# A transformer block whose TensorE takes turns between attention rows, weighted sums and one dense product, with fewer re-layouts and other places for two small steps

## The chip, the cores and the metric

The kernel runs on one core of a Trainium2 chip. The metric is device time in microseconds (us) from the first to the last instruction's end as the launch sees it, the median of several runs. A core has five engines with instruction streams of their own, which wait for each other by semaphores: TensorE (PE: matmuls, with the loading of the stationary operand, PEld, beside them), VectorE (DVE), ScalarE (ACT), GpSimd (POOL) and SyncE (SP, which here only starts transfers). Sixteen DMA engines move data. PSUM, where TensorE writes, has eight banks of 128 partitions by 512 floats.

## The reference, cut

```python
# S=2048 rows, D=640, H=32 heads of Dh=20, window W=256, F=1536; float32; inputs about 0.05 * randn
def _A_ref(x, wqkv, wo):                       # x is already layer-normalised
    q, k, v = (x @ wqkv).reshape(B, S, 3, H, Dh).transpose(2, 0, 3, 1, 4)
    scores = einsum("bhqd,bhkd->bhqk", q, k) * Dh ** -0.5
    mask = (i - j >= 0) & (i - j < W)
    p = softmax(where(mask, scores, -1e9))
    return einsum("bhqk,bhkd->bhqd", p, v).transpose(0, 2, 1, 3).reshape(B, S, D) @ wo
def _B_ref(x, w_gate, w_up, w_down):
    return (gelu(x @ w_gate) * (x @ w_up)) @ w_down
h  = x + _A_ref(layernorm(x), wqkv, wo)
h2 = h + _B_ref(layernorm(h), w_gate, w_up, w_down)
```

## The kernel before, in words

**Precision.** Every operand of a dense product is split into a high and a low half in float16, and a product is the sum of three matmuls (high by high, high by low, low by high). With 640 = 5 x 128 rows of contraction, a product into one bank (`products`, L538) is 15 matmuls: 256 columns wide for q and k, 320 for v and the output projection `wo`, 512 for gate and up.

**Tiles.** The 2048 rows are 16 blocks of 128; two blocks are a chunk of 256 columns, so eight chunks. q and k come out of their products transposed (features on partitions). `qk_out` (L717) splits them into halves, and ScalarE's queue writes them to DRAM (`qk<-qks`). `stack` (L737) reads them back in the layout that attention needs: for each parity of head, at partitions 0 and 64, three groups of 20 partitions (the 20 features of a head), for q high, high, low and for k high, low, high, so that one contraction over 60 partitions gives the three-term product. These re-layouts are `qT<-qk` (two buffers, one per chunk, taken by turns) and `kT<-qk` (a ring of six blocks), both started in SP's queue. For chunk c of 2 and more the one for q waits until block 2c-3 has had its weighted sums (`scored`), since it overwrites the q of two chunks ago.

**Attention.** A block of 128 queries has eight units: a unit is a parity of head and four heads, against up to three blocks of keys. For each unit:

- `maxima` (L792): 12 matmuls with queries on partitions (`ps<-kT,qT`, 60 rows of contraction); then VectorE masks one block of keys by a predicated copy and reduces the maxima to `mxs` (`max_out`, L886). When all eight units have them, `max_rows` and `max_transpose` turn the maxima into two more rows of q (`mT`, written by two transfers `qT<-mT` in ScalarE's queue).
- `scores` (L804): 12 matmuls with keys on partitions (`ps<-qT,kT`, 62 rows, so that the maximum is subtracted), the exponential on ScalarE (`pt<-ps,esc`), and the causal masks on GpSimd.
- weighted sums (`value_lane`, L948): 12 matmuls `ps<-pt,v` into bank 7 (`PV`), a quarter of the bank for each unit, with a column of ones that yields the softmax's denominator. After four units ScalarE copies the bank to `oT`, and `normalise` (L973) turns it by four transposes into a free bank, where VectorE takes the reciprocal (`rec`) and multiplies (`o32`). After eight units `o_transpose` splits `o32` in halves (`turned`, L506: high by ScalarE into `sph`, low by VectorE into `spl`) and two transposing transfers `oh<-sph`, `ol<-spl` in SP's queue give the operand of `wo_block`. `turned` does the same for the layer norms' outputs (`xh`, `xl`, and `h0h`, `h0l` before the feed-forward part).

A row stretch (`row_lane`, L874) is one unit's maxima and another unit's scores, of opposite parity, whose matmuls alternate; it takes six of the PSUM banks (`SETS`: 0 to 2 and 3 to 5), and VectorE, or ScalarE, frees its three when it has read them. Bank 6 is for dense products.

**What sets the order.** All instructions are written out at build time by a planner. Each piece of work is a generator (a lane) that says on which engine its next instruction runs and from when it may; a model of the engines' times (`Clock`) says when that is. At each step the main loop (from L1335) takes the first lane of a list that may start. The list `order` puts small work first (outputs, transposes, side work) and then the three lanes that fill TensorE: `rows`, `values` and `dense` (the products of q, k, v, `wo`, and later the feed-forward part). Which of the three comes first depends on the share of dense work done against the share of scores done (`ahead`), and weighted sums come early where the last matmul was one of a row stretch (`nc.mode == "row"`). A lane keeps its place only for one instruction, so a product of 15 matmuls may be cut anywhere by the others. All instructions go through one helper, so in the profile they bear its line L192; what they are is told by the names of their tiles.

Of the kernel before, what the change touches and what calls it, by code (L numbers as in the profile page):

```python
# [22 lines left out]
NB = S // P  # L23
# [222 lines left out]
def block_kernel(ctx: ExitStack, tc: tile.TileContext, x, wqkv, wo, wg, wu, wd, out):  # L246
# [18 lines left out]
    def at_bank(i):  # L265
        return ps8[:, i * 512:(i + 1) * 512]
# [18 lines left out]
    def bank(kind, dt=F32):  # L285
        b = pick(kind)[1]
        held[b] = kind
        ap = at_bank(b)
        return ap if dt == F32 else ap.bitcast(dt)

    def done(ap):
        del held[nc.box(ap)[1][2] // BANK]
# [32 lines left out]
    FFBACK = dict(split_lane=0.4, scale_lane=0.4, chunk_lane=0.3)  # L325
    EARLY = 0.6
    PACE = 1.0

    def need(*reads, slots=(), when=None, eng="tensor"):

# [6 lines left out]
    def pe(*reads, slots=(), when=None):  # L337
        return ("tensor",), need(*reads, slots=slots, when=when)

    def on(eng, *reads, when=None, after=None):  # L340
        f = need(*reads, when=when, eng=eng)
        if after is not None:
            return (eng,), lambda: max(f(), nc.others(after, eng))
        return (eng,), f
# [161 lines left out]
    def turned(src, lane, to, dst=None, when=None):  # L506

        yield on("scalar", src, when=lambda: not opened["parts"] and (not when or when()))
        opened["parts"] += 1
        hi, lo = (nc.tile(lnp, [P, D], F16, n, 1) for n in ("sph", "spl"))  # L510
        nc.scalar.copy(hi, src)
        yield on("vector", hi)
        nc.vector.tensor_tensor(lo, src, hi, op=ALU.subtract)
        if dst:
            to = dst()
        for o, i in zip(to, (hi, lo)):
            yield ("sync",), need(i, eng="sync")
            nc.sync.dma_start_transpose(o, i)
        opened["parts"] -= 1
# [18 lines left out]
    def products(n, term, ready=None, at_=None):  # L538


        ps = [at_[0]] if at_ else []
        col = at_[1] if at_ else 0

        def start(i):
            if ready and not ready(i):
                return INF
            t = nc.ready([x for ab in term(i) for x in ab], "tensor")
            return t if ps else max(t, room("mm"))

        for i in range(n):  # L550
            yield ("tensor",), lambda i=i: start(i)
            if not ps:
                ps.append(bank("mm"))
            m = term(i)
            for k, (l, r) in enumerate(m):
                if k:
                    yield pe()
                o = ps[0][:, col:col + r.free_size()]
                nc.tensor.matmul(o, l, r, start=(i == 0 and k == 0),
                                 stop=(i == n - 1 and k == len(m) - 1))  # L560
                pos["dense"] += r.free_size() * 3 // len(m)
        return o

    ffk = const.tile([P, FG, 5], F32, name="ffk")
# [172 lines left out]
    def stack(c, which, d):  # L737
        yield ("sync",), need(when=lambda: pos["consts"] and (c < 2 or B[2 * c - 3].scored),
                              eng="sync")
        if which == 0:  # L740
            C[c].qT = at("qT", [P, H // 2, CW], F16)
            for b in (2 * c, 2 * c + 1):
                B[b].mx = at("mxs", [P, H], F32, 4)
            to = C[c].qT
        else:
            s = 2 * c % RK
            to = kT[:, :, s:s + 2, :].rearrange("p i r n -> p i (r n)")
        for par in range(2):
            for m, i in enumerate(((0, 0, 1), (0, 1, 0))[which]):
                rows = slice(64 * par + DH * m, 64 * par + DH * m + DH)  # L750
                if c > 1:
                    yield ("sync",), lambda: nc.moved["sync"] - PACE
                nc.sync.dma_start(to[rows], d[i].rearrange("(a d i) n -> a d i n", a=2,
                                                           d=DH)[par])
        C[c].stacked += 1
        if C[c].stacked == 2:
            for b in (2 * c, 2 * c + 1):
                maxq.extend((b, u ^ 1) for u in range(H // 4))
            maxq.sort(key=lambda x: (x[0], x[1] // 2))
# [114 lines left out]
    def row_lane():  # L874
        while True:
            yield ("tensor",), row_need
            gens = []
            for s, (f, x) in enumerate(row):
                (maxq if f is maxima else scoreq).remove(x)
                gens.append(f(*x, row_set(s)))  # L880
            for ops in zip_longest(*gens):
                for op in ops:
                    if op:
                        nc.tensor.matmul(*op, start=True, stop=True)
# [63 lines left out]
    def value_lane():  # L948

        while True:  # L950
            yield pe(when=lambda: valq and B[valq[0][0]].v == 2 and pos["ones"])
            j, u = valq.popleft()
            b = B[j]
            pt = b.pt.pop(u)
            ks = window(j)
            n = len(ks)
            order = [1, 0, 2] if n == 3 else list(range(n))
            yield pe(pt[:, 3 - n:3], pv[:, u % 4, :])
            for k, i in enumerate(order):
                for c in range(4):  # L960
                    nc.tensor.matmul(pv[32 * c:32 * c + DH + 1, u % 4, :],
                                     vring[ks[i] % RV][:, 4 * u + c, :], pt[:, 3 - n + i, c, :],
                                     start=(k == 0), stop=(k == n - 1))
            pos["values"] += 1
            if u % 4 == 3:
                yield on("scalar", pv, when=lambda: pos["normal"] == 2 * j + u // 4)
                oT = at("oT", [P, 4, P], F32, 1)
                nc.scalar.copy(oT, pv)
                tps.append(normalise(j, u // 4, oT))
            if u == 7:  # L970
                b.scored = True

    def normalise(j, half, oT):  # L973
        b = B[j]
        yield pe(oT, slots=["tp"], when=lambda: j == 0 or half or B[j - 1].normal)
        if half == 0:
            b.o32 = at("o32", [P, H, DH], F32, 1)
        t = bank("tp")
        OR = 3 * 32 + DH + 1
        for u4 in range(4):  # L980
            nc.tensor.transpose(t[:, u4 * P:u4 * P + OR], oT[:OR, u4, :], ident[:OR, :OR])
        pos["normal"] += 1
        tv = t.rearrange("p (h e) -> p h e", e=32)
        rec = at("rec", [P, 16], F32)
        yield on("vector", t)
        nc.vector.reciprocal(rec, tv[:, :, DH])
        yield on("vector", rec)
        nc.vector.tensor_tensor(b.o32[:, 16 * half:16 * half + 16, :], tv[:, :, 0:DH],
                                rec[:, :, None].to_broadcast([P, 16, DH]), op=ALU.mult)
        done(t)  # L990
        pos["over"] = j == NB - 1 and half
        if half:
            tps.append(o_transpose(j))

# [340 lines left out]
    while dense.alive or sides or side or outs or tasks:  # L1335
        while side:
            back, gen = side.pop(0)
            sides.append(Lane(gen, back))
        while tps:
            trans.append(Lane(tps.pop(0), OUT))  # L1340
        while tasks:
            outs.append(Lane(tasks.pop(0), OUT))
        att_lanes = [rows, values]
        ahead = pos["dense"] / DENSE - pos["score"] / (H // 4) - TARGET
        early = [l for l in sides if l.gen.__name__ == "x_lane"] if not B[XF].ready else []
        if not W["v"].ready:
            att_first = maxq or nc.t["vector"] < nc.t["tensor"]
        else:
            att_first = ahead > 0
        if W["o", 0].ready:  # L1350
            outs.sort(key=lambda l: l.gen.__name__ == "low")
        if nc.mode == "row":
            early = [values] + early
        elif len(valq) < 2 and row_need() < INF:
            att_lanes = [rows]
        order = (early + outs + trans + sides
                 + (att_lanes + [dense] if att_first else [dense] + att_lanes))
        for lane in order:
            if lane.alive and lane.start(now):
                break  # L1360
        else:
            now += 0.03
            idle += 1
            assert idle < 20001, "nothing can be issued"
            continue
        idle = 0
        lane.step()
        trans = [l for l in trans if l.alive]
        outs = [l for l in outs if l.alive]
        sides = [l for l in sides if l.alive]  # L1370
# [48 lines left out]
```

## Time and profile before

| what | value |
|---|---|
| three runs | 1147.69, 1149.43, 1153.9 us; median 1149.43 |
| the profiled execution: time, span | 1152.97 us, 1151.0 us |
| mean granted TensorE clock | 0.966 |
| busy: PE, DVE, ACT, POOL | 1009.4 (88%), 636.6 (55%), 386.8 (34%), 195.3 us (17%) |
| attention beside projections | about 100 to 750 us of the span |
| feed-forward part (gate, up, down), from about 750 us on | 401 us |

Busy time counts an engine's work, not its waiting. A line of the waits gives: the operation that waited, an arrow, what ended its waiting, then the total in us, the number of times, and the longest. A line of the groups gives the operation with its tiles and shapes, the count, the busy time and the mean of one in ns, and then the idle time of the engine ahead of these operations with what ended most of it. DMA share is that of all sixteen engines. A line of the chain gives a start, a length and what filled it.

### The profile page before, as it was taken

Reading aid. Unit: us, or ns where it says so; the run is one execution under the profiler, and the core shown is the slowest. Engines: PE = TensorE matmul, PEld = TensorE weight load, DVE = VectorE, ACT = ScalarE, POOL = GpSimd, SP = SyncE. Lnnn points to the kernel's source line nnn. Section 1 sums busy time; section 2 is a strip of 40 time slices with the busy share of each in tenths; the row PEclk is TensorE's granted clock in tenths of the full one; section 3 lists DMA queues with packets and bytes.
Section 4 is the critical chain, followed back from the end, with each engine's and each line's share of the span. In section 5 each row is a group of like instructions: output and inputs, shape, how many; then the busy total and the mean of one; then the engine's idle time right before and its main releaser. Section 6 shows DMA issues by size and latency. Waiting matters only on the chain.

```text
span 1151.0 us, 24750 instructions
## 1 busy us (share of the span) xinstructions
PE 1009.4 (88%) x10722; PEld 642.7 (56%) x10722; DVE 636.6 (55%) x1185; ACT 386.8 (34%) x480; POOL 195.3 (17%) x298
## 2 busy tenths in 40 slices
PE   3898877888758588797899988899999999999998
PEld 2686555665536466465665554355554555455546
DVE  8966996777748376166267724982452245222223
ACT  2422445555525135245155554431111112111110
POOL 8100212333323013123033130000000000000000
PEclk9998899899989889899899999999999999999999
DMA  8536466245453402602505212520320023001001
GB/s 296 122 102 167 120 175 139 64 107 94 85 90 79 108 26 59 137 14 50 137 14 174 70 13 77 173 59 1 97 42 1 1 92 46 1 1 46 1 1 47
DMA packets 117004, 90.01 MB, mean 78 GB/s; under 512 B 59872, under 2 KB 95968, under 8 KB 115936
## 3 DMA queue, kind: packets, MB, share of 16 engines
q1 hardware_dynamic: 93792, 77.68, 26.6%
q10 hardware_dynamic: 23104, 10.75, 3.7%
q8 instruction: 84, 1.38, 0.5%
q14 instruction: 24, 0.20, 0.1%
HBM read 54.07 MB, written 20.97 MB: 65 GB/s over the span
## 4 chain that ended last, share of the span: by engine, by line
PE 68%; DVE 14%; DMA 9%; ACT 4%; issue 3%; SPq 1%; ACTq 1%; POOL 0%; DVEq 0%
PE ps L192 68%; DVE mxs L192 4%; DVE ps L192 2%; ACT pt L192 2%; DMA kT<-qk 2%; DVE am L192 2%; DMA qk<-qks 1%; DMA qT<-mT 1%; DMA xh<-sph 1%; DMA ol<-spl 1%; SPq L192 1%; DVE qks L192 1%; ACTq L192 1%; DMA xl<-spl 1%; DVE ht L192 1%
## 5 line engine op out<-in xcount | busy, mean ns | idle before, releaser
L192 ACT ACTIVATE pt<-ps,esc 128x1536 f32<-128x1536 f32 (+2 forms) x128 | 185.8, 1459 | 186.3 <-PE ps L192 166.1
L192 POOL TENSOR_SCALAR_AFFINE_SELECT pt<-pt 128x512 f32<-128x512 f32 x240 | 153.2, 660 | 460.1 <-ACT pt L192 459.9
L192 DVE TENSOR_REDUCE mxs<-ps 128x4 f32<-128x1024 f32 (+1 forms) x128 | 150.8, 1185 | 2.5
L192 PE MATMUL ps<-kT,qT 60*128 60x128 f16 x1440 | 101.1, 223 | 54.6 <-DVE mxs L192 27.9
L192 DVE COPY_PREDICATED ps<-tri,ps 128x512 f32<-128x512 int32 x112 | 77.1, 692 | 94.9 <-PE ps L192 94.8
L192 DVE SCALAR_TENSOR_TENSOR gel<-ps,ffk,gel 128x512 f32<-128x512 f32 x48 | 36.0, 750 | 144.7 <-PE ps L192 144.6
L192 PEld LDWEIGHTS <-qT 60*128 60x128 f16 x1440 | 82.0, 97 | 55.5 <-issue 50.7
L192 PE MATMUL ps<-pt,v 128*21 128x128 f32 x2880 | 105.6, 278 | 3.7 <-ACT oT L192 2.4
L192 DVE SCALAR_TENSOR_TENSOR ht<-ps,ffk,ht 128x320 f32<-128x320 f32 x96 | 52.8, 550 | 87.4 <-PE ps L192 87.4
L192 PE MATMUL ps<-qT,kT 62*128 62x128 f16 x1440 | 98.1, 221 | 3.1 <-DMA qT<-mT 1.7
L192 ACT ACTIVATE gel<-ps,ffk 128x512 f32<-128x512 f32 x48 | 32.9, 686 | 192.5 <-PE ps L192 188.6
L192 PEld LDWEIGHTS <-kT 62*128 62x128 f16 x1440 | 76.4, 96 | 36.1 <-issue 33.8
L192 PEld LDWEIGHTS <-ah 128*128 128x128 f16 x768 | 74.9, 98 | 32.0 <-issue 1.5
L192 PEld LDWEIGHTS ps<-pt,v 128*21 128x21 f32 x2880 | 68.9, 101 | 23.9 <-issue 5.5
L192 PEld LDWEIGHTS <-gu 128*128 128x128 f16 x480 | 46.3, 98 | 55.9 <-issue 2.4
L192 ACT CAST ah<-gel 128x512 f16<-128x512 f32 x48 | 29.6, 617 | 130.9 <-DVE gel L192 130.8
L192 PE MATMUL ps<-hTh,gu 128*128 128x512 f16 x240 | 71.9, 379 | 0.0
L192 PE MATMUL ps<-w3h,oh 128*128 128x320 f16 x160 | 52.3, 327 | 16.9 <-DMA oh<-sph 8.7
L192 PE MATMUL ps<-xh,w0h 128*128 128x256 f16 x200 | 56.9, 284 | 6.4 <-ACT w0h L192 1.9
L192 PE MATMUL ps<-xh,w1h 128*128 128x256 f16 x200 | 56.1, 281 | 6.9 <-DVE qks L192 4.8
L192 PE MATMUL ps<-w2h,xh 128*128 128x320 f16 x160 | 49.8, 311 | 10.2 <-ACT v L192 8.0
L192 PE MATMUL ps<-xh,w1l 128*128 128x256 f16 x200 | 56.2, 281 | 1.9 <-DVE w1l L192 1.8
(206 smaller groups left out, 2136.4 us busy)
## 6 DMA issues: line engine op xcount, KB each, us to landing
qk<-qks ACTq DMA_DIRECT2D x64, 128.0 KB
qT<-qk SPq DMA_DIRECT2D x48, 160.0 KB
kT<-qk SPq DMA_DIRECT2D x48, 160.0 KB
ht<-in_x_dram SPq DMA_DIRECT2D x16, 320.0 KB
h_dram<-ht SPq DMA_DIRECT2D x16, 320.0 KB
ht<-h_dram SPq DMA_DIRECT2D x16, 320.0 KB
out_dram<-ht SPq DMA_DIRECT2D x15, 320.0 KB
wst<-in_wd_dram SPq DMA_DIRECT2D x12, 320.0 KB
```

The costliest lines, as they stand in the source:

```text
L192: r = real(*args, **kw)
```

## The change

It has four parts.

1. **Order.** The planner's main loop gets a new rule. While a dense product is open (`pos["open"]`), its matmuls come first, so that all 15 stand in a row; after a row stretch come weighted sums, then a dense product, then rows; after weighted sums a dense product, then rows. If a whole product has been done since the last stretch (`pos["since"]`) and rows could start within 2 us (`SOON`) by the model, only rows and weighted sums may start.
2. **Normalisation in bank 7.** The four transposes of `normalise` go back into the bank of the weighted sums that they come from. So the next unit's weighted sums wait until VectorE has multiplied (`pos["normal"]` is counted up there, not behind the transposes).
3. **Low halves by GpSimd.** In `turned` the subtraction that gives `spl` moves from VectorE to GpSimd. This holds for the layer norms' outputs too.
4. **Fewer re-layouts.** In `stack`, for each operand and parity, three transfers of 20 partitions become one of 40 partitions and one of 20. For q the one of 40 takes high and low from DRAM, and the third group takes high; for k the one of 40 takes high twice by a broadcast, and the third group takes low. The order of the three groups changes with it (q: high, low, high; k: high, high, low), which leaves the same three products.

```diff
+    SOON = 2.0
...
     def turned(src, lane, to, dst=None, when=None):
...
         nc.scalar.copy(hi, src)
-        yield on("vector", hi)
-        nc.vector.tensor_tensor(lo, src, hi, op=ALU.subtract)
+        yield on("gpsimd", hi)
+        nc.gpsimd.tensor_tensor(lo, src, hi, op=ALU.subtract)
...
     def products(n, term, ready=None, at_=None):
...
                 ps.append(bank("mm"))
+            pos["open"] = 1
             m = term(i)
...
+        pos["open"] = 0
+        pos["since"] += 1
         return o
...
     def stack(c, which, d):
...
+        dv = d.rearrange("m (a d i) n -> a m d i n", a=2, d=DH)
         for par in range(2):
-            for m, i in enumerate(((0, 0, 1), (0, 1, 0))[which]):
-                rows = slice(64 * par + DH * m, 64 * par + DH * m + DH)
+            for m, n in ((0, 2), (2, 1)):
+                rows = slice(64 * par + DH * m, 64 * par + DH * (m + n))
+                if which == 0:
+                    src = dv[par, 0:n]
+                else:
+                    src = dv[par, m // 2:m // 2 + 1].to_broadcast([n, DH, H // 2, CW])
                 if c > 1:
                     yield ("sync",), lambda: nc.moved["sync"] - PACE
-                nc.sync.dma_start(to[rows], d[i].rearrange("(a d i) n -> a d i n", a=2,
-                                                           d=DH)[par])
+                nc.sync.dma_start(to[rows], src)
...
     def row_lane():
...
+            pos["since"] = 0
...
     def value_lane():
...
-            yield pe(pt[:, 3 - n:3], pv[:, u % 4, :])
+            yield pe(pt[:, 3 - n:3], pv[:, u % 4, :],
+                     when=lambda: pos["normal"] == 2 * j + u // 4)
...
-                yield on("scalar", pv, when=lambda: pos["normal"] == 2 * j + u // 4)
+                yield on("scalar", pv)
...
     def normalise(j, half, oT):
...
-        yield pe(oT, slots=["tp"], when=lambda: j == 0 or half or B[j - 1].normal)
+        yield pe(oT, pv, when=lambda: j == 0 or half or B[j - 1].normal)
...
-        t = bank("tp")
+        t = at_bank(PV)
...
-        pos["normal"] += 1
...
-        done(t)
-        pos["over"] = j == NB - 1 and half
+        pos["normal"] += 1
+        if j == NB - 1 and half:
+            pos["over"] = 1
+            del held[PV]
...
-        att_lanes = [rows, values]
-        ahead = pos["dense"] / DENSE - pos["score"] / (H // 4) - TARGET
...
         if not W["v"].ready:
             att_first = maxq or nc.t["vector"] < nc.t["tensor"]
+            turn = [rows, values, dense] if att_first else [dense, rows, values]
+        elif pos["open"]:
+            turn = [dense, values, rows]
+        elif nc.mode == "row":
+            turn = [values, dense, rows]
+        elif nc.mode == "col":
+            turn = [dense, rows, values]
         else:
-            att_first = ahead > 0
...
-        if nc.mode == "row":
-            early = [values] + early
-        elif len(valq) < 2 and row_need() < INF:
-            att_lanes = [rows]
-        order = (early + outs + trans + sides
-                 + (att_lanes + [dense] if att_first else [dense] + att_lanes))
+            turn = [rows, values, dense]
+        if W["v"].ready and not pos["open"] and pos["since"] and row_need() < nc.t["tensor"] + SOON:
+            turn = [rows, values]
+        order = early + outs + trans + sides + turn
```

`nc.mode` is "row" when the last matmul was one of a row stretch, "col" when it was a weighted sum. From chunk 1 to chunk 7 TensorE's order after the change is nearly everywhere 24 matmuls of a stretch, 12 of weighted sums, 15 of one product; before, 1 to 123 dense matmuls stand between two stretches, in pieces of any length. Its stream changes from one kind of work to another 479 times where it did 507 times, up to the feed-forward part.

On TensorE, what stands ahead of the first maxima of block 8 (chunk 4). Before, with the numbers of the tiles (`w2h`, `w2l` are v's weights, `xh`, `xl` the layer-normalised rows):

```order
L192 LDWEIGHTS xh_669
L192 MATMUL ps8_73<-w2l_479,xh_669 128x320
L192 LDWEIGHTS xl_670
L192 MATMUL ps8_73<-w2h_478,xl_670 128x320
L192 LDWEIGHTS qT_4271
L192 MATMUL ps8_73<-kT_109,qT_4271 128x128
L192 LDWEIGHTS kT_109
L192 MATMUL ps8_73<-qT_3268,kT_109 128x128
```

After (`w0h`, `w0l` are q's weights):

```order
L192 LDWEIGHTS w0h_227
L192 MATMUL ps8_73<-xl_4388,w0h_227 128x256
L192 LDWEIGHTS w0l_228
L192 MATMUL ps8_73<-xh_4387,w0l_228 128x256
L192 LDWEIGHTS qT_4458
L192 MATMUL ps8_73<-kT_109,qT_4458 128x128
L192 LDWEIGHTS kT_109
L192 MATMUL ps8_73<-qT_3413,kT_109 128x128
```

What moved: the work ahead is now a whole product of q for a later chunk, where before it was a part of a product of v.

On SP's queue, the re-layouts of q and k for chunk 4 and the transposing transfers among them. Before:

```order
L192 DMA qT<-qk_2210 20x4096
L192 DMA_TRANSPOSE oh<-sph 128x5x128
L192 DMA_TRANSPOSE ol<-spl 128x5x128
L192 DMA qT<-qk_2210 20x4096 x5
L192 DMA kT<-qk_2741 20x16x256 x6
```

After:

```order
L192 DMA qT<-qk_2027 40x1x4096
L192 DMA_TRANSPOSE xl<-spl 128x5x128
L192 DMA xt<-in_x_dram 128x640
L192 DMA_TRANSPOSE oh<-sph 128x5x128
L192 DMA qT<-qk_2027 20x4096
L192 DMA qT<-qk_2027 40x1x4096
L192 DMA_TRANSPOSE ol<-spl 128x5x128
L192 DMA qT<-qk_2027 20x4096
L192 DMA kT<-qk_2375 40x16x256
L192 DMA kT<-qk_2375 20x16x256
L192 DMA kT<-qk_2375 40x16x256
L192 DMA kT<-qk_2375 20x16x256
```

What moved: twelve re-layouts are eight, four of them of 40 partitions, and `oh` and `ol`, which stood behind one re-layout, now stand behind one and behind three. In both orders the first of them waits for `scored`.

More of the change, by code (lines that the diff above doesn't have):

```diff
@@ L1342, in block_kernel @@
             outs.append(Lane(tasks.pop(0), OUT))
-        att_lanes = [rows, values]
-        ahead = pos["dense"] / DENSE - pos["score"] / (H // 4) - TARGET
         early = [l for l in sides if l.gen.__name__ == "x_lane"] if not B[XF].ready else []
+        if W["o", 0].ready:
+            outs.sort(key=lambda l: l.gen.__name__ == "low")
         if not W["v"].ready:
             att_first = maxq or nc.t["vector"] < nc.t["tensor"]
-        else:
-            att_first = ahead > 0
-        if W["o", 0].ready:
-            outs.sort(key=lambda l: l.gen.__name__ == "low")
-        if nc.mode == "row":
-            early = [values] + early
-        elif len(valq) < 2 and row_need() < INF:
-            att_lanes = [rows]
-        order = (early + outs + trans + sides
-                 + (att_lanes + [dense] if att_first else [dense] + att_lanes))
+            turn = [rows, values, dense] if att_first else [dense, rows, values]
[5 more added lines that the diff above has]
+            turn = [dense, rows, values]
+        else:
+            turn = [rows, values, dense]
+        if W["v"].ready and not pos["open"] and pos["since"] and row_need() < nc.t["tensor"] + SOON:
+            turn = [rows, values]
+        order = early + outs + trans + sides + turn
         for lane in order:
```

## The prediction

> **What bounds the kernel now.** I read the page first, then windows by stage, then what TensorE (PE) waits for, then single turns of the chain, and at last the DMA rows. Of the page, the span and TensorE's busy share in its 40 slices:
>
> ```profile
> span 1151.0 us, 24750 instructions
> ...
> PE   3898877888758588797899988899999999999998
> ```
>
> The digits end in nines: the last third is TensorE at work without a gap, and the middle, where attention is interleaved with projections, has sevens, eights and two fives. Three windows (length, then busy time and count of PE, PEld, DVE, ACT, POOL, then granted clock, DMA share, GB/s) give sizes:
>
> ```profile
> 0.00:100.00 100.00, 78.62 (x641) 61.28 (x642) 78.41 (x194) 30.65 (x56) 29.60 (x36) 0.98 0.58 168
> 100.00:750.00 650.00, 533.12 (x7850) 362.98 (x7848) 416.25 (x705) 293.82 (x329) 158.55 (x250) 0.94 0.39 94
> 750.00:1151.00 401.00, 397.61 (x2235) 218.42 (x2232) 141.98 (x289) 62.35 (x95) 7.14 (x12) 1.00 0.11 30
> ```
>
> After 750 TensorE is the bound (397.61 of 401) and the order there changes little: I cost it at nothing. From 100 to 750 TensorE idles 650 - 533.12 = 117 us. What ended its idle times there (total, times, longest):
>
> ```profile
> PE ps L192 <- DVE mxs L192: 29.0, 32, 2.3
> PE ps L192 <- DMA kT<-qk: 25.0, 4, 8.0
> PE ps L192 <- ACT v L192: 10.1, 11, 2.3
> PE ps L192 <- DVE qks L192: 9.0, 11, 2.2
> PE ps L192 <- DMA oh<-sph: 8.7, 3, 3.6
> PE ps L192 <- ACT oT L192: 5.9, 8, 2.2
> PE ps L192 <- DVE ht L192: 5.5, 6, 1.3
> PE ps L192 <- DMA ol<-spl: 5.4, 4, 2.2
> ```
>
> So two waits lead: the maxima on VectorE, and the landing of the re-laid k (and q) from DRAM, which is already late in four chunks of eight.
>
> **The turns.** A row stretch holds both sets of three banks until VectorE has masked (copy) and reduced its maxima. In the chain, where stretches follow each other with little between:
>
> ```profile
> 309.16 0.88 PE ps L192 x24
> ...
> 310.75 1.24 DVE mxs L192
> ...
> 312.03 0.88 PE ps L192 x24
> ```
>
> From 309.16 to 312.03 is 2.87 us a turn, the floor that VectorE sets. Two windows that hold one whole turn each without a gap (24 row matmuls, 12 weighted sums as 24 records, then 14 products of 256 columns or 11 of 320):
>
> ```profile
> 189.04:192.27 3.23, 3.23 (x63) 2.57 (x63) 2.52 (x3) 2.60 (x3) 1.45 (x3) 1.00 0.55 146
> 296.36:299.52 3.16, 3.16 (x60) 2.24 (x60) 1.92 (x2) 1.54 (x1) 1.18 (x3) 1.00 0.02 5
> ```
>
> And of the timeline the first and last of a run of products of each width (start, length):
>
> ```profile
> 190.72 0.27 PE L192 MATMUL ps<-xl,w0h 128*128 128x256 f16 x1
> ...
> 192.03 0.27 PE L192 MATMUL ps<-xl,w0h 128*128 128x256 f16 x1
> ...
> 422.13 0.30 PE L192 MATMUL ps<-w2h,xh 128*128 128x320 f16 x1
> ...
> 422.81 0.30 PE L192 MATMUL ps<-w2h,xl 128*128 128x320 f16 x1
> ```
>
> Twelve steps in 1.31 us are 0.109 each, five in 0.68 are 0.136. With the 15 products that the new order places in nearly every turn, a turn lasts 3.23 + 0.11 = 3.34 us (q, k) or 3.16 + 4 x 0.136 = 3.70 us (v, output). Both are over 2.87, so TensorE covers the wait for the maxima. Of the 29.0 us I leave 8, for some ten turns that get no whole product (0.7 each): **-21**. The small waits for a bank or a copy (v 10.1, qks 9.0, oT 5.9, ht 5.5) are 30.5; between 0 and all of it goes; products now come one at a time, with a stretch between to empty the bank, but ScalarE and VectorE still empty it behind the exponentials: half, **-15**. The transposes oh and ol (14.1 together) I leave as they are: they stand in SP's queue among the re-layouts that follow.
>
> **The re-layouts, the term that decides.** Per chunk and operand six transfers of 20 partitions become four: for each parity one of 40 partitions, whose source in DRAM has an outermost dimension of 2 (high and low for q; the same rows twice, by a broadcast, for k), and one of 20. Bytes stay the same. What a transfer's shape does to its rate can be read from three windows: loads of 128 partitions; the transfer of mT alone, which writes 2 partitions from a source of 32; and k's re-layout alone, 20 partitions, with TensorE idle:
>
> ```profile
> 2.00:6.00 4.00, 0.00 (x0) 0.00 (x0) 1.98 (x6) 0.08 (x1) 3.88 (x3) 1.00 0.96 296
> 136.55:136.90 0.35, 0.35 (x12) 0.35 (x7) 0.16 (x1) 0.15 (x1) 0.16 (x1) 1.00 0.11 23
> 399.50:400.50 1.00, 0.00 (x0) 0.00 (x0) 0.00 (x0) 0.00 (x0) 0.00 (x0) 0.50 0.59 168
> ```
>
> 0.96 of 16 engines is all; 0.59 is 9.4, so ten, as 20 splits ten ways; 0.11 is 1.8, so two, though mT's other side has 32 rows. The smaller outermost count sets the number of engines, and in the merged transfer that count is 2. That is an inference: no row here has its small count on the source side. On one side or the other it is worth this. A busy engine moves 168 / (0.59 x 16) = 17.8 GB/s in k's 512-byte pieces and 296 / (0.96 x 16) = 19.3 in longer ones. A merged transfer is 40 x 4096 x 2 bytes = 328 kB: on two engines 9.2 us (k) and at most 8.5 (q); a single one, 164 kB at 168 GB/s, 1.0. A chunk: 2 x 9.2 + 2 x 8.5 + 4 x 1.0 = 39.4 us, all through the same two engines. To this come issue and landing; of the chain, k's last transfer of a chunk, alone:
>
> ```profile
> 326.48 3.81 DMA kT<-qk
> ```
>
> 3.81 less the 1.0 of moving is 2.8, so 42 us from the first issue. Fewer issues on SP gain nothing: what ends the wait is the landing.
>
> How much of the 42 is covered? The first transfer overwrites the q of two chunks ago, so it waits for the last scores of block 2c-3. In the new order the first maxima of block 2c stand six turns behind them, of the odd parity, whose transfers come last: 4 x 3.34 + 2 x 3.70 = 20.8 us, 21. Left: 21 us a chunk, 19 taken, as q's runs of 8 kB should go faster than the 2560-byte ones behind the 19.3. Chunks 2 to 7: 6 x 19 = **+114**; it takes the place of the **-25.0**. Behind that wait stands everything on TensorE, in order, so nothing covers it; VectorE, ScalarE and GpSimd run dry with it. In SP's queue the transposes oh and ol of the running block stand among the merged transfers and move behind them on those two engines; the output products that wait for them take up a part of the same 19. Ends: 0 if ten engines serve the merged form (2 x 4 transfers' bytes at 168 GB/s are 12 us, inside 21), and 6 x 47 = 280 if the engines are as slow as with several transfers in flight:
>
> ```profile
> 484.00:485.00 1.00, 1.00 (x9) 0.72 (x8) 0.00 (x0) 0.00 (x0) 0.00 (x0) 1.00 0.76 131
> ```
>
> 131 / (0.76 x 16) = 10.8 GB/s, 15.2 us a merged transfer. I stay at the lower price: with two engines at work there is less to contend with, as in the 0.59 window.
>
> The Trainium skill, "DMA: Bandwidth & Descriptors", section "Why a DMA increments its semaphore by 16 and not by 1", says that the engines are the largest number up to 16 that divides the outermost dimension of both sides; its section "Rules for kernel authors" warns of a leading zero-stride broadcast of c copies. The trace agrees for the destination (1.8 engines busy for mT); it has no row for the source. By that rule the sum is the one below; by the narrower reading, in which the destination's 40 partitions decide, it is the first rival's 1071.
>
> **The rest.** The clock: 0.50 in the window at 399.50 shows that a wait of some us halves it. 0.94 over 650 us means 78 us at half; six long waits cost a few us each on resuming where four long and many short ones did: **+5**, between -10 and +15.
>
> Low halves and normalisation:
>
> ```profile
> L192 DVE TENSOR_TENSOR spl<-o,sph 128x640 f16<-128x640 f32 x16 | 13.7, 855 | 5.3 <-ACT sph L192 4.4 <-DMA xl<-spl 0.9
> ...
> L192 POOL TENSOR_SCALAR_AFFINE_SELECT pt<-pt 128x512 f32<-128x512 f32 x240 | 153.2, 660 | 460.1 <-ACT pt L192 459.9
> ...
> L192 DVE TENSOR_TENSOR o<-ps,rec 128x320 f32<-128x320 f32 x32 | 15.5, 484 | 0.5
> ...
> L192 DVE RECIPROCAL rec<-ps 128x16 f32<-128x16 f32 x32 | 8.0, 250 | 14.3 <-PE ps L192 14.2
> ```
>
> VectorE sheds 40 low halves of 0.85 us, 34 us; worth nothing beyond the -21, since TensorE covers VectorE. On GpSimd one costs 0.83 us by the select (660 x 640 / 512) to twice that with its two inputs. GpSimd is busy 195 of 1151 us by the windows, and the products of the transposes stand a turn behind; only the last block shows it: **+1**. The weighted sums now wait for the normalisation of the last four units: 0.25 + 0.48 and hand-overs, 0.9 us, 32 times, 0 to 29 us. In the order a product or its rest and a stretch stand between, 1.3 us at least, so **+2**. Fewer changes of TensorE's tiling (479 runs of one kind, 507 before) are inside the rounding.
>
> **Sum.** The profiled execution took 1152.97 us (span 1151.0), 3.5 over the median of the three runs. 1153 - 21 - 15 - 25 + 114 + 5 + 1 + 2 = 1214; as a median, 1210.
>
> **Rivals.**
> - Ten engines serve the merged transfers (the destination's 40 decides). For it: nothing in the trace excludes it. Against: mT's two. Then the stack is inside the 21 us: 1153 - 21 - 15 - 25 - 10 (oh, ol) - 10 (clock) + 3 = 1075, median 1071: faster. The turning point against the time before is a wait of 9 us a chunk (six of them make up for 21 + 15 + 25 less 8), a stack of 30 us.
> - Two engines, but more cover (turns nearer 4 us, faster runs of q): 9 us a chunk left, 54 instead of 114: 1153 - 21 - 15 - 25 + 54 + 8, median 1150.
> - Two engines at the contended rate: 280 instead of 114, 1375.
> - Ten engines, and the bank of the weighted sums is the new wait: 1071 + 29 + the 15 of the small waits = 1115.
>
> **Chances.** Forecast 0.66 (own range 1170 to 1260), ten engines 0.15, more cover 0.12, contended 0.04, bank 0.03. The range takes all but the first and third rival: 1110 to 1285. Faster by over 0.5% (what three runs can tell from no change): 0.15 + 0.03 + 0.04 of the cover case, 0.22; within, 0.03; slower, 0.66 + 0.04 + 0.05, 0.75.
>
> **What would show it.** Right: PE waits for kT<-qk and qT<-qk of some 110 us in six or more places, a DMA share near 0.12 while a merged transfer runs alone, waits for mxs under 10 us. Wrong: a share near 0.6 there and landings within 4 us of issue; then the time is near 1071. Waits of TensorE for rec or o before weighted sums would mean the bank; waits for spl, GpSimd.

## The result and the profile after

The changed kernel takes 1231.47 us (median of four runs, 1228.5 to 1234.64), the kernel before 1149.8 beside it: a ratio of 1.0706, 95% interval 1.0666 to 1.0747. The forecast was 1210 with a range of 1110 to 1285, slower with a chance of 0.75.

The page of the kernel after, with span, busy times, TensorE's slices and the second line of the chain's shares:

```profile
span 1229.1 us, 24727 instructions
...
PE 1014.9 (83%) x10722; PEld 648.1 (53%) x10722; DVE 622.6 (51%) x1145; ACT 387.4 (32%) x480; POOL 248.6 (20%) x338
...
PE   4568588759668487797855899789999999999998
...
PE ps L192 55%; SPq L192 8%; DMA kT<-qk 6%; DMA qT<-qk 5%; DMA qk<-qks 3%; DVE mxs L192 2%; DMA xh<-sph 1%; DVE am L192 1%; DVE ps L192 1%; ACT pt L192 1%; DMA ol<-spl 1%; DMA oh<-sph 1%; DMA xl<-spl 1%; DMA wsl<-in_wo_dram 1%; POOL spl L192 1%
```

TensorE's busy time is 1014.9 us against 1009.4; its idle time is 214.2 (1229.1 - 1014.9) against 141.6. So of 78 us of span, 73 are waiting. The second and third slice (of 31 us each) read 5 and 6 where before they read 8 and 9: the loss begins in the ramp. In the chain SP's own issuing (SPq) has 8% and the re-layouts 11%. The same line of the page before:

```profile
PE ps L192 68%; DVE mxs L192 4%; DVE ps L192 2%; ACT pt L192 2%; DMA kT<-qk 2%; DVE am L192 2%; DMA qk<-qks 1%; DMA qT<-mT 1%; DMA xh<-sph 1%; DMA ol<-spl 1%; SPq L192 1%; DVE qks L192 1%; ACTq L192 1%; DMA xl<-spl 1%; DVE ht L192 1%
```

The same three stages by windows, and what ended TensorE's waits in the middle one:

```profile
0.00:100.00 100.00, 58.29 (x434) 44.65 (x435) 65.76 (x170) 26.75 (x48) 29.66 (x36) 0.88 0.42 137
100.00:830.00 730.00, 561.22 (x8068) 386.16 (x8067) 417.15 (x706) 298.58 (x337) 194.92 (x278) 0.89 0.40 88
830.00:1230.00 400.00, 395.38 (x2224) 217.32 (x2221) 139.68 (x271) 62.10 (x95) 23.99 (x24) 1.00 0.11 30
```

```profile
PE ps L192 <- DMA kT<-qk: 47.6, 4, 14.5
PE ps L192 <- DMA oh<-sph: 27.7, 3, 16.2
PE ps L192 <- DVE mxs L192: 20.7, 18, 6.2
PE ps L192 <- ACT oT L192: 17.7, 8, 9.1
PE ps L192 <- issue: 9.9, 3, 4.2
PE ps L192 <- DVE qks L192: 8.9, 7, 4.5
```

The feed-forward part is as long as before. The first 100 us hold 434 matmuls where before there were 641. In the middle, k's re-layout is waited for up to 14.5 us at a time, where before it was 8.0. The chain of one such wait, chunk 2, whose first re-layout of q SP issued at 218.86:

```profile
220.08 16.04 DMA qT<-qk
236.12 0.02 issue
236.13 8.45 SPq L192
244.59 0.04 issue
244.63 0.94 SPq L192
245.58 0.04 issue
245.62 14.78 DMA kT<-qk
```

From 218.86 to 260.40 are 41.5 us: the prediction had 42. Read the same way, the stacks of chunks 3, 4 and 6 took 43.1, 41.8 and 42.0. How many engines move is read from windows in it. First while q's merged transfer is under way (chunk 3), then while k's is (chunk 2, TensorE idle):

```profile
309.00:313.00 4.00, 1.33 (x40) 0.81 (x32) 0.00 (x0) 0.52 (x1) 0.00 (x0) 1.00 0.12 50
...
250.00:256.00 6.00, 0.00 (x0) 0.00 (x0) 0.00 (x0) 0.00 (x0) 0.00 (x0) 0.53 0.14 39
```

0.12 and 0.14 of sixteen are 1.9 and 2.2 engines, and 39 GB/s are 17.4 for each busy engine (39 / (0.14 x 16)), where the prediction took 17.8. Before, the same data of k moved on 9.4 engines (0.59 in the window that the prediction shows).

### The profile page after: what moved, and what is told of

Its sections match the earlier page's. It is cut to its first block, busy times and chain, and to the rows that moved or that the text cites. A ratio compares the mean times of both kernels' runs of the same rounds, so it can differ in the third digit from the quotient of the medians.

```text
span 1229.1 us, 24727 instructions
## 1 busy us (share of the span) xinstructions
PE 1014.9 (83%) x10722; PEld 648.1 (53%) x10722; DVE 622.6 (51%) x1145; ACT 387.4 (32%) x480; POOL 248.6 (20%) x338
## 4 chain that ended last, share of the span: by engine, by line
PE 55%; DMA 20%; DVE 10%; SPq 8%; ACT 2%; issue 2%; POOL 1%; ACTq 0%; DVEq 0%; POOLq 0%
PE ps L192 55%; SPq L192 8%; DMA kT<-qk 6%; DMA qT<-qk 5%; DMA qk<-qks 3%; DVE mxs L192 2%; DMA xh<-sph 1%; DVE am L192 1%; DVE ps L192 1%; ACT pt L192 1%; DMA ol<-spl 1%; DMA oh<-sph 1%; DMA xl<-spl 1%; DMA wsl<-in_wo_dram 1%; POOL spl L192 1%
## 5 line engine op out<-in xcount | busy, mean ns | idle before, releaser
L192 POOL TENSOR_SCALAR_AFFINE_SELECT pt<-pt 128x512 f32<-128x512 f32 x240 | 150.4, 649 | 418.7 <-ACT pt L192 416.5
L192 PE MATMUL ps<-kT,qT 60*128 60x128 f16 x1440 | 107.6, 225 | 70.6 <-DMA kT<-qk 47.6
L192 PEld LDWEIGHTS <-qT 60*128 60x128 f16 x1440 | 86.1, 98 | 88.5 <-issue 59.5
L192 PE MATMUL ps<-pt,v 128*21 128x128 f32 x2880 | 109.2, 283 | 10.4 <-issue 3.9
L192 PE MATMUL ps<-qT,kT 62*128 62x128 f16 x1440 | 105.0, 225 | 9.9 <-ACT pt L192 6.1
L192 PEld LDWEIGHTS <-kT 62*128 62x128 f16 x1440 | 82.2, 98 | 24.6 <-issue 24.4
L192 PE MATMUL ps<-w3h,oh 128*128 128x320 f16 x160 | 52.1, 326 | 28.8 <-DMA oh<-sph 27.7
L192 DVE SCALAR_TENSOR_TENSOR qks<-ps,qks 128x512 f16<-128x512 f32 (+1 forms) x48 | 28.8, 599 | 69.6 <-ACT qks L192 69.4
L192 PE MATMUL ps<-xh,w0l 128*128 128x256 f16 x200 | 57.3, 287 | 1.0 <-DVE w0l L192 1.0
```

Source lines behind the costliest of these rows:

```text
L192: r = real(*args, **kw)
```

## The experiments

All ratios are to the kernel before, timed on the same chip in the same rounds (its medians there 1146.75 to 1148.26 us). In the traces the changed kernel and experiments 1, 4, 5, 6, 10 and 12 have the same 10722 matmuls in the same order.

**1. Six small transfers again.**

```diff
 # stack(), from the changed kernel
-            for m, n in ((0, 2), (2, 1)):
...
+            for m, i in enumerate(((0, 0, 1), (0, 1, 0))[which]):
+                rows = slice(64 * par + DH * m, 64 * par + DH * m + DH)
...
+                nc.sync.dma_start(to[rows], d[i].rearrange("(a d i) n -> a d i n", a=2, d=DH)[par])
```

> The changed kernel with one part undone: the re-layouts are again six transfers of 20 partitions for each operand and chunk; TensorE's instruction order stays as in the changed kernel, matmul for matmul. Theory (the merged transfers run on two of sixteen DMA engines, and all of the loss is there, in the ramp too): about 1071 us, 1055 to 1095; waits of TensorE for kT<-qk under 25 us, none over 8, and the first maxima start near 68 us instead of 90. Rival (the new order, the bank of the weighted sums or GpSimd's low halves cost the time): stays above 1150 us, and the first maxima stay near 90 us.

Measured: 1080.8 us, ratio 0.9418 (0.9365 to 0.9471). The same order of TensorE's matmuls is 151 us faster. The other three parts of the change are thus worth 67 us, and the merge costs more than twice that. Its page and waits:

```profile
span 1082.3 us, 24776 instructions
...
PE 988.9 (91%) x10722; PEld 635.5 (59%) x10722; DVE 620.9 (57%) x1145; ACT 387.2 (36%) x480; POOL 247.7 (23%) x338
```

```profile
PE ps L192 <- DVE mxs L192: 20.1, 19, 5.2
PE ps L192 <- ACT oT L192: 8.0, 7, 2.0
PE ps L192 <- DMA kT<-qk: 6.2, 4, 2.8
PE ps L192 <- DMA oh<-sph: 6.1, 3, 4.3
PE ps L192 <- DVE qks L192: 2.5, 5, 0.8
```

k's landing costs 6.2 us in all, against 47.6 with the merge.

**2. The merge alone, in the kernel before.** The edit is the change's part in `stack` and nothing else.

> The kernel before with only the merged re-layouts. Theory: the stack of a chunk takes 42 us from first issue to last landing as in the changed kernel, against 27 us (176.8 to 204) for the six small ones in the order before: 15 us more for each of chunks 2 to 7, 90 us, and the 45 us that the changed kernel lost before the first maxima of block 2: 1149 + 135 = 1285 us, 1230 to 1330. Rival (the merged form costs only with the new order, which leaves less work behind it): under 1180 us.

Measured: 1276.41 us, ratio 1.1131 (1.1081 to 1.1182): 129 us from one part of the diff, with the old rule. The planner counts the merged transfers, so the order that it writes is not matmul for matmul that of the kernel before.

**3. One transfer of 40 partitions with another outermost dimension.**

```diff
-        dv = d.rearrange("m (a d i) n -> a m d i n", a=2, d=DH)
+        dv = d.rearrange("m (a d i) n -> a d m i n", a=2, d=DH)
...
+                moves = [(slice(p, p + 2 * DH), dv[par, :, 0:2]),               # q: high, low in turn
+                         (slice(p + 2 * DH, p + 3 * DH), dv[par, :, 0])]
...
+                moves = [(slice(p, p + 2 * DH, 2), dv[par, :, 0]),              # k: even rows
+                         (slice(p + 1, p + 2 * DH, 2), dv[par, :, 0]),          # k: odd rows
+                         (slice(p + 2 * DH, p + 3 * DH), dv[par, :, 1])]
```

> The changed kernel, with the merged transfer of q written so that its source's outermost dimension is the 20 features and its inner one high and low (rows high, low, high, low in turn, and k's rows to match); same 40 partitions, same bytes, same number of transfers of q; k in six transfers of 20 partitions. Theory (the smaller outermost count of the two sides sets the engines): ten engines, landing of one merged transfer of q within 5 us, time as with six small transfers, 1055 to 1095 us. Rival (a transfer of 40 partitions or of 328 kB is slow whatever its dimensions): q's merged transfers take 9 us or more each, and the time is that of the version with only q merged as in the change, at least 15 us above that with six.

Measured: 1067.95 us, ratio 0.9311 (0.9267 to 0.9354), the fastest of all. A window while q's merged transfer of chunk 1 is under way there:

```profile
79.00:81.00 2.00, 2.00 (x21) 1.79 (x20) 0.69 (x1) 0.60 (x1) 0.00 (x0) 1.00 0.70 195
```

0.70 is 11 engines (a few other transfers move too), 195 GB/s against 50 in the window at 309. So the cause is neither the 40 partitions nor the 328 kB nor the number of transfers. (TensorE's order is not quite that of experiment 1 here; experiment 12 holds it.)

**4. Only q merged as in the change, k in six.**

> The changed kernel with only q's re-layouts merged (outermost dimension 2, no broadcast) and k's again six transfers of 20 partitions; TensorE's order unchanged. Theory (two engines, whether the source is broadcast or not): q's two merged transfers take 16 us in sum instead of some 3, half of what the change lost; between the version with six and the changed kernel: 1090 to 1160 us. Rival (the broadcast of k, which reads the same rows twice, is what is slow): within 10 us of the version with six small transfers for both.

Measured: 1137.52 us, ratio 0.9925 (0.9901 to 0.9949): 57 us above experiment 1, with no broadcast anywhere.

**5. The ramp apart.** The changed kernel with the first two chunks in six transfers. (Those chunks keep the old order of the three groups of rows, so scores between chunks 1 and 2 pair other halves and come out wrong; shapes and TensorE's instructions are the same.)

```diff
+        if c < 2:
+            ...                        # six transfers of 20 partitions
+        else:
             for m, n in ((0, 2), (2, 1)):
```

> The changed kernel with the re-layouts of chunks 0 and 1 in six transfers of 20 partitions and those of chunks 2 to 7 merged as in the change; TensorE's order unchanged. Theory (the loss before the first maxima of block 2 is the merged transfers of the first two chunks, which nothing covers, and it stays to the end): the first maxima of block 2 start near 138 us as in the version with six instead of 176.8, and of the changed kernel's 1231 us 38 go: 1193 us, 1175 to 1210. Rival (what is lost at the start is won back later, since work then stands behind the waits): 1215 us or more.

Measured: 1189.88 us, ratio 1.0359 (1.0319 to 1.0399): 42 us less than the changed kernel. Its page:

```profile
span 1187.5 us, 24743 instructions
...
PE 1007.4 (85%) x10722; PEld 643.6 (54%) x10722; DVE 622.3 (52%) x1145; ACT 387.2 (33%) x480; POOL 248.8 (21%) x338
```

**6. The ramp's merge alone**: chunks 0 and 1 merged as in the change, all others in six. The edit against the changed kernel:

```diff
-            for m, n in ((0, 2), (2, 1)):
+            for m, n in ((0, 2), (2, 1)) if c < 2 else ((0, 1), (1, 1), (2, 1)):
...
-                    src = dv[par, 0:n]
+                    src = dv[par, m % 2:m % 2 + n]
```

> The version with six small transfers, with the merged transfers in chunks 0 and 1 alone; TensorE's order unchanged. Theory (the ramp has no work to cover the transfers and what is lost there stays): 1081 + 40 = 1121 us, 1108 to 1133. Rival (won back later): under 1100 us.

Measured: 1120.61 us, ratio 0.9777 (0.9746 to 0.9808), 40 us above experiment 1. So the loss adds up: 40 to 42 for chunks 0 and 1, and 1189.88 - 1080.8 = 109 for chunks 2 to 7.

**7 to 9. The other parts, undone on experiment 1**: low halves back on VectorE; the transposes of `normalise` back in a free bank; both (the new order alone is left).

> The version with six small transfers, with the low halves back on VectorE. Theory (TensorE covers VectorE, so its 34 us are worth nothing): within 10 us of the version with six, 1071 to 1091 us, waits for mxs near 20 us. Rival (VectorE is still a bound in the turns): 15 to 34 us more, 1096 to 1115, in waits for mxs.

> The version with six small transfers, with the normalisation's transposes in a free bank again, as before the change. Theory (the wait of the weighted sums for the bank costs about 2 us): 1070 to 1090 us. Rival (a product now stays open till its end and holds the dense bank, so that the transposes find no free bank, the only oT stays taken, and the next weighted sums and scores come late): 15 us more or over, above 1095 us, with waits for oT or pt.

> The kernel before with the new order alone: six small transfers, low halves on VectorE, normalisation in a free bank. Theory (the order is the whole gain): 1070 to 1095 us, as the version with six. Rival (the order gains only with the bank or with GpSimd's low halves): 1100 to 1150 us.

Measured: 1102.84 us, ratio 0.9612 (0.9579 to 0.9645); 1095.19, 0.9540 (0.9507 to 0.9573); 1103.24, 0.9611 (0.9578 to 0.9644). The order alone gives about 45 us. Each of the two small steps alone adds 8 or nothing; both together add 22. All three expectations missed. In the first and the third the time is in the rival's range, but the first rival's sign did not come: waits for mxs are 18.0 us, not more than the 20.1 of experiment 1. The second is at the edge of the rival's range (above 1095), and its sign, waits for oT, did not come either (8.4 us, 8.0 in experiment 1).

**10 and 11. Engine and order of the low halves apart.** In the first, VectorE runs the low halves, but the planner counts them as GpSimd's, so the order is that of experiment 1. In the second GpSimd runs them, but they are counted as VectorE's, so the order is that of experiment 7. The edit of the first:

```diff
-        nc.gpsimd.tensor_tensor(lo, src, hi, op=ALU.subtract)
+        nc.vector.real.tensor_tensor(lo, src, hi, op=ALU.subtract)
+        nc.issue("gpsimd", nc.gpsimd.cost("tensor_tensor", lo, [src, hi]), [src, hi], [lo])
```

> The version with six small transfers in its own order on every engine's stream of matmuls, but with the low halves run by VectorE: the planner still counts them as GpSimd's work, so TensorE's order is that of the version with six, not that which the planner makes when it knows. Theory A (the work taken off VectorE is worth the 22 us by itself): 1096 to 1108 us. Theory B (the 22 us come from the order that the planner makes when the low halves are VectorE's): 1073 to 1088 us.

> The counterpart: TensorE's order of the version with low halves on VectorE, but GpSimd runs them. Theory A (taking the work off VectorE is what counts): 1075 to 1090 us. Theory B (the order counts): 1096 to 1108 us.

Measured: 1090.09 us, ratio 0.9509 (0.9479 to 0.9539), between the two theories; and 1101.86, 0.9610 (0.9583 to 0.9636), as theory B has it. With one order VectorE's work costs 9 us, and TensorE's waits for the maxima grow from 20.1 to 26.8:

```profile
PE ps L192 <- DVE mxs L192: 26.8, 28, 5.4
```

With the other order GpSimd's help is worth nothing (1101.86 against 1102.84). That order itself costs 21 us where GpSimd runs the halves (1101.86 against 1080.8) and 13 where VectorE does (1102.84 against 1090.09).

**12. Experiment 3's transfers in experiment 1's order.**

> The version with q's high and low rows in turn in one transfer on ten engines, but with TensorE's order of the version with six (the planner counts six transfers). Theory A (the saved transfers of q are worth nothing, and the 13 us between those two versions come from the planner's order): 1075 to 1087 us. Theory B (fewer transfers land sooner): 1060 to 1073 us, and waits for kT<-qk under 2 us where the version with six has 6.2.

Measured: 1078.52 us, ratio 0.9397 (0.9369 to 0.9426), the same as experiment 1 within the intervals, though waits for kT<-qk are 2.4 us against 6.2. Theory A: 10.6 of the 13 us by which experiment 3 leads are gone when the order is held, so they came from the planner's order; fewer transfers gave nothing that can be told from zero. With experiment 4 this makes the pair that tells most: TensorE's order is the same, q's transfers are as many and as large, k has six in both, and only the source's first dimension differs (20 or 2) with the place of rows that follows from it: 1078.52 against 1137.52 us.

## Why the prediction was right, and where it was not

By its terms:

| term | forecast | measured | by |
|---|---|---|---|
| re-layouts, chunks 2 to 7 | +114 | +109 | 5 less 1 |
| re-layouts, chunks 0 and 1 | not in the sum | +40 | 6 less 1 |
| all else (-21 - 15 - 25 + 5 + 1 + 2) | -53 | -67 | 1 against before |
| sum | +61 | +82 | |

**The term that decided held, in mechanism and size.** The stack takes 41.5 us (42 forecast). A loss of 19 us a chunk was forecast. The order is the same in the changed kernel and in experiment 1, so the stretch from the first maxima of one odd block to those of the next (3 to 5, up to 13 to 15) can be compared: the changed kernel takes 16.0 to 22.3 us longer, 17.9 in the mean of the six.

Two things in this are luck. That 42 came out to half a microsecond is one: at the 50 GB/s of the window at 309 a merged transfer of q needs 6.6 us (an estimate, 328 kB / 50 GB/s) where 8.5 at most was taken, and the transposes oh and ol, which were not in the 42, were issued in between. The other is the make-up of the 109 us: in the profiles of experiments 5 and 1 (105.2 us of span) TensorE's idle time grows by 86.7 and its busy time by 18.5, where the forecast had all 114 as waiting.

The clause that was called an inference, that the smaller outermost count decides on the source's side too, is shown by experiments 4 and 12 and by the windows of 0.12 and 0.70. The rule of the Trainium skill that stood beside it ("DMA: Bandwidth & Descriptors", section "Why a DMA increments its semaphore by 16 and not by 1") says so for both sides, and the runs agree (1.9 and 2.2 engines where the source counts 2, 9.4 where both sides count 20). The Trainium skill's section "Rules for kernel authors", of the same page, gives a leading broadcast as its example of a small outermost dimension; experiment 4 loses 57 us without one. The first rival, ten engines, had 1071 as its time; kernels whose re-layouts run on ten engines took 1068, 1079 and 1081 (experiments 3, 12 and 1). The contended rate did not come: 17.4 GB/s for each engine.

**Left out of the sum: the ramp.** The step that failed is "Chunks 2 to 7: 6 x 19". The first two chunks are not in it and no reason is given. But there TensorE's order has too little to cover their transfers: 434 matmuls in the first 100 us, where before there were 641. The chain after, in the ramp:

```profile
39.39 14.42 DMA qk<-qks
...
53.94 1.83 DMA qk<-qks
...
63.30 9.83 SPq L192
73.13 0.05 issue
73.18 7.33 DMA xt<-in_x_dram
```

A store of q and k landed after 14.42 us, while merged transfers of q were under way (the next store, issued when they had landed, took 1.83). By the trace's semaphore records, which mark the landing of each piece, fourteen of the first store's sixteen pieces had landed at 41.20 us; the last two came at 53.00 and 53.81, next to the two pieces of q's second merged transfer (52.70 and 53.51). And a load of x stood in SP's queue behind a held re-layout. Both feed TensorE there. The first maxima of block 2 start at 176.8 us, against 131.5 before and 138.3 in experiment 1, and nothing wins this back later (experiment 6).

**Turns: right to three hundredths, in the two that were read.** Forecast 3.34 and 3.70 us with a product of 256 and of 320 columns. Two turns of experiment 1, the second with q's product:

```profile
214.59:218.29 3.70, 3.70 (x64) 2.64 (x63) 3.58 (x8) 2.17 (x2) 2.41 (x3) 1.00 0.91 123
412.88:416.19 3.31, 3.31 (x65) 2.64 (x65) 1.97 (x3) 2.14 (x2) 1.64 (x4) 1.00 0.38 75
```

**The wait for the maxima: too little left.** Of 29.0 us 8 were to stay, ten turns with no whole product at 0.7 each; 20.1 stay in experiment 1. Nine turns have no matmul of a product there, and three of them show the price:

```profile
PE ps L192 <- DVE mxs L192: 3.3, 3, 1.3
```

(window 486 to 496 us): 1.1 each where 0.7 was taken; the waits behind all nine are 9.0 us. The longest wait, 5.2, stands in the ramp, which the forecast left out here too. So -9 stands where -21 was forecast.

**The clock: the right number by luck.** After, TensorE's busy time is 5.5 us more than before (forecast +5), with a granted clock of 0.928 against 0.966. But this is the balance of two larger changes: in experiment 1 it is 20.5 less (988.9 against 1009.4, granted clock 0.984), where the first rival had 10 less, and the merge adds 26.0 to that (1014.9 against 988.9). The 20.5 and the small waits (v, qks, oT, ht: 30.5 before, 12.8 in experiment 1, so -18 for -15) make up for the maxima in "all else".

**The low halves and the bank: the step "worth nothing" failed.** VectorE's 34 us were put at nothing, the bank at +2. Together they gain 22 us (0.9418 against 0.9611). The reason given, that TensorE covers VectorE, does not hold in full: in experiment 1's order VectorE's relief is worth 9 us (experiment 10), 6.7 of them in waits for the maxima. The order that the planner writes when it counts on GpSimd is itself worth 13 to 21 (experiments 7, 10 and 11). For the bank, worth 14 us beside GpSimd's low halves (1095.19 against 1080.8), order and bank were not taken apart. Which part of an order does it stays open: in experiment 7 the waits for oh and ol are 14.6 us (8.2 and 6.4) against 8.6 (6.1 and 2.5), and the clock is 0.976 against 0.984, which is not all of 22.

**What would show it: half right.** Waits named kT and qT were to be 110 us in six places. They are 47.6 in four; the rest of the loss stands under other names, which are small where the merge is undone: oh<-sph 27.7 (6.1 in experiment 1), oT 17.7 (8.0), qks 8.9 (2.5), and issue 9.9. The text had said that oh and ol move behind the merged transfers and take up a part; it had not let that change the sign to look for. The share near 0.12 came; waits for mxs under 10 us did not (20.7). TensorE did not wait for spl or rec, and for o, the bank's other sign, it waited 1.7 us, near the +2 that was put on it:

```profile
PE ps L192 <- DVE o L192: 1.7, 6, 0.5
```

## What to carry to other kernels

Before transfers are merged to save issues, look at the outermost dimension of both sides of the merged form: here 2 in place of 20 took the merged re-layouts from ten engines to two. Turning the dimensions round gave q's merge at no loss, and at no gain either. Price a transfer's shape in the ramp too, where little work covers it. And where a planner writes the order, the worth of moving an operation to another engine is not its duration: here 9 us came from the engine, and 13 to 21 from what the planner then wrote.

## What the hardware showed that was not expected

SP is held at the issue itself while merged transfers are under way. A stretch of the chain after:

```profile
627.63 19.22 SPq L192
646.84 0.06 issue
646.90 0.02 SPq L192
646.92 0.04 issue
646.95 6.18 DMA oh<-sph
653.13 0.05 issue
653.18 6.85 PE ps L192 x73
```

The issue of one re-layout of k took 19.22 us, and the transpose of oh could only be issued behind it; TensorE's wait of 16.2 us for oh is this. In the trace after, 29 of SP's 302 issues of transfers last over 1.5 us, 191.9 us in sum; in that before, 10 of 334, 17.1 us; in experiment 1, with TensorE's order of the changed kernel, 16 of 334, 31.0 us, the longest 2.5. So the merged transfers cost twice here: by landing late, and by keeping what stands behind them in SP's queue from being issued. How much may be under way before SP is held, these runs do not tell.
